# Power tables in a kernel that mixes attention with a state-space convolution: one product straight into the table, the other added to it by a GpSimd transfer

## The chip, the cores and the metric

The kernel runs on one core of a Trainium2 chip. The metric is the device time of one execution in microseconds (us), lower is better; of several timed executions the median counts. TensorE is called PE here, VectorE DVE, ScalarE ACT, GpSimd POOL, and SyncE SP. Each engine takes its instructions in order from its own queue and waits on semaphores of the others.

## The reference, cut to what matters

```python
g = sigmoid((x * gate_w).sum(-1, keepdims=True))       # x is 2048 x 512
a = softmax_attention(x, wqkv, wo)                      # 32 heads of 16, 2048 keys
logdA, dB = dt * (A_re + 1j*A_im), dt * (B_re + 1j*B_im)  # 512 channels x 128 states
P = jnp.exp(logdA[:, :, None] * l)                      # powers 0..2047 of lambda = exp(logdA)
K = einsum("dn,dnl,dn->dl", Cc, P, dB).real             # a long filter for every channel
b = causal_convolution(x, K) + x * Dskip
out = g * a + (1 - g) * b
```

The filter is applied in chunks of 64 time steps. For that the kernel needs, for each channel and state, the complex powers of lambda from 0 to 63 (times a constant): the power table, real and imaginary part, 512 channels x 128 states x 64 powers.

## The kernel before, in words

**A planner.** The program is not written out as a list. `record` builds it from threads (Python generators) that yield segments with an engine, a cost in us and a priority. For each of the NG = 683 groups of the attention (loop at line 1716) the planner places one exponential on ACT, then the score products of the next group, and then `Sched.fill` (line 372) puts in every segment of other threads that fits by its model of the engines: `op` (line 199) and `dma` (line 224) carry modelled cost and latency, `ready` (line 156) adds a margin of DMARG = 2.4 us (or PTM = 5.0) to the end of a transfer before anything that needs it is placed. The result is a fixed order for each engine; on the chip only semaphores and that order count. A first pass finds the first and last group in which each tile is used, `place` (line 526) packs the tiles into SBUF (tiles whose spans do not meet may share bytes), and a second pass replays the log with the waits that the packing adds.

**Attention.** A group is three score tiles of 128 keys x 512 queries in one of two PSUM tensors SC0 and SC1 (`qk`, line 890). `ex` (line 905) applies exp on ACT to the whole group (128x1536) or, where the third tile is given to DVE, to two tiles (128x1024). There are 2048 tiles. A *set* (`decide`, line 799; `bits`, 941; `batch`, 951) is one quad of four tiles that DVE takes instead of ACT, one tile from each of four successive groups: for each tile one operation from PSUM (line 945, tile DZ), and for each set two operations over all four tiles (line 956, tiles DU and DZ). A set starts only if its group lies in one of the windows WIN (first group, last group, sets in flight, key lists), if the key tile is in the lists VKT, and if DVE has been idle enough: by the model, idle time of DVE since the last sets (at most DVCAP = 2.0 us is kept) must reach the price that DVQ names. The price before is 0.5 us until the mark S15, then 1.0 until scan0, then 0.5 until scan1, then 0.0.

**The state-space part** fills the gaps. `params` (line 1074) makes powers of lambda and the factors D16, D32, D48 (one tile for each quarter of the channels, every factor stored twice in a row). `base` (line 1173) makes the powers 0 to 15 of each quarter in tile B16. `table` (line 1211) goes through 8 pairs of blocks of 32 channels. For a pair it copies B16 into the table tile PT (two copies, line 1227), and for each of the three factors and both parts it makes two products into tt1 and tt2 (line 1234) and their sum or difference into PT (line 1239): 2 + 3 x 2 x 3 = 20 operations of DVE. These product and sum operations go through the helper `tt`, so the profile has them on line 1006. Then SP stores both blocks of PT to DRAM (ptd, line 1244). The next pair waits for the marks K of both blocks, which `kstage` (line 1265) sets: PE multiplies PT with weights (line 1273), DVE copies the result to Kst (1277, 1278), SP stores it (1282). `qload` (line 1252) loads the stored table transposed, `sstage` (line 1288) makes the chunk states SG (it may start at the group SGAT = 175 for the first half of the channels, at 315 for the second; POOL clears the head of SG, line 1296), `scan` (line 1317) runs the recurrence over 32 chunks on DVE in two halves that end with the marks scan0 and scan1, and `ystage` (line 1384) makes the output of the convolution from SG and the table. S15 is the end of `sstage` of the last block. At the end of `emit` (line 244) SP waits for the last value of each DMA semaphore (line 272).

The line of the table that matters, with `ti` one of tt1 and tt2:

```python
tt("DVE", ti,                       B16 part xr, D part yr, ALU.mult ...)      # twice
tt("DVE", PT at 16 * m, t1, t2,     ALU.add if part else ALU.subtract ...)     # once
```

Of the kernel before, what the change touches and what calls it, by code (L numbers as in the profile page):

```python
# [2 lines left out]

# [10 lines left out]
P = 128  # L14
S = 2048
# [12 lines left out]
XAT = "base0"  # L28
# [10 lines left out]
SGAT = (175, 315)  # L39
# [50 lines left out]
class Prog:  # L90
# [133 lines left out]
    def dma(self, eng, fn, R=(), W=(), c=.45, lat=3.0, m=DMARG):  # L224
# [4 lines left out]
        k = self.dnext  # L229
        self.dnext = (k + 1) % NDSEM  # L230
# [13 lines left out]
    def emit(self, nc, es):  # L244
        sem = {e: es.enter_context(nc.semaphore("s_" + e)) for e in ("PE", "ACT", "DVE", "POOL")}
        dsem = [es.enter_context(nc.semaphore(f"s_d{k}")) for k in range(NDSEM) if self.dn[k]]
# [9 lines left out]
        def stream(eng):  # L256
            def body(e):
# [11 lines left out]
                if eng == "SP":  # L269
                    for k in range(NDSEM):  # L270
                        if self.dn[k]:
                            e.wait_ge(dsem[k], 16 * self.dn[k])
# [142 lines left out]
def declare(nc, es):  # L415
# [64 lines left out]
    for n in (16, 32, 48):  # L480
        for k in range(4):
            sb(f"D{n}.{k}", 4 * P)
# [8 lines left out]
    sb("tt1", 2 * CB * 16)  # L491
    sb("tt2", 2 * CB * 16)
# [33 lines left out]
def place(nc, bufs):  # L526

    base, end = (nc.sbuf_base + 31) // 32 * 32, nc.sbuf_usable_end
    sbs = [b for b in bufs.values() if b.kind == "sb" and b.first is not None]

    def fit(order):
        done, top = [], base
        for b in order:
            n = (b.nbytes() + 31) // 32 * 32
            busy = sorted((o.lo, o.hi) for o in done if o.first <= b.last + 1 and b.first <= o.last + 1)
            at = base
            for lo, hi in busy:
                if at + n <= lo:
                    break
                at = max(at, hi)  # L540
            b.lo, b.hi = at, at + n
            top = max(top, b.hi)
            done.append(b)
        return top

    best, seed = None, 1
    for k in range(400):
        def rank(b):
            nonlocal seed
            seed = (seed * 1103515245 + 12345) % 2 ** 31  # L550
            w = seed / 2 ** 31 * (0 if k < 2 else .8)
            return (-(b.last - b.first > 300) if k % 2 else 0, -b.nbytes() * (1 + w * 2) * (b.last - b.first + 20) ** (w if k >= 2 else 0))
        order = sorted(sbs, key=rank)
        top = fit(order)
        if best is None or top < best[0]:
            best = (top, order)
    k = 0
    while best[0] > end and k < 12000:
        k += 1
        order = list(best[1])  # L560
        for _ in range(1 + k % 3):
            seed = (seed * 1103515245 + 12345) % 2 ** 31
            b = order.pop(seed // 7 % len(order))
            seed = (seed * 1103515245 + 12345) % 2 ** 31
            order.insert(seed // 7 % (len(order) + 1), b)
        top = fit(order)
        if top <= best[0]:
            best = (top, order)
    assert best[0] <= end, (best[0] - end, live(sbs))
    fit(best[1])  # L570
# [41 lines left out]
def record(nc, p, B, ins):  # L612
# [461 lines left out]
    def params():  # L1074
# [69 lines left out]
        for o, x, y in (("L16", "L8", "L8"), ("L32", "L16", "L16"), ("L48", "L16", "L32"), ("MU", "L32", "L32")):  # L1144
            yield from cmul("DVE", o, x, y)
            if o != "MU":
                for k in range(4):
# [3 lines left out]
                       [(l, 0)], [(d, 0)], c=.34)  # L1151
        sch.mark("D48")
# [58 lines left out]
    def table():  # L1211
        yield ("AFTER", "D48")
        t1, t2 = B["tt1"], B["tt2"]
        H10 = dv(1024, 2)
        for pb in range(NBLK // 2):
# [8 lines left out]
            W = [(PT, 0, blks[0]), (PT, 1, blks[1])]  # L1224
            for i in range(2):
                yield ("DVE", .4)
                op("DVE", lambda v, i=i, b0=b0, B16=B16: v.tensor_copy(PT(i * PTN, [[CB * T, 2], [T, CB], [1, 16]]),
                                                                     B16(b0 + i * CB * 16, [[2048, 2], [16, CB], [1, 16]])), bk, [W[i]], c=.34)
# [589 lines left out]
```

## Time and profile before

| what | value |
|---|---|
| median of the timed executions | 838.77 us (838.6 to 840.81, 3 runs) |
| span of the profiled execution, first to last instruction | 837.7 us; the page gives no other time of that execution |
| median less that span | 1.07 us |
| PE busy | 698.3 us, 83% |
| DVE busy | 783.3 us, 94%, 1344 instructions |
| ACT busy | 819.1 us, 98%, 695 instructions |
| POOL busy | 11.0 us, 1%, 13 instructions |
| mean granted clock of TensorE | 0.991 |
| transfers | 94.90 MB, 49.6% of the 16 DMA engines' span on the SP queue |

An operation's mean duration in the rows includes the part that overlaps with its neighbour on the same engine; busy time divided by the count is what one costs in a row of many.

### The profile page before, as it was taken

What the parts mean: (1) busy time and instruction counts of PE and PEld (TensorE: products, weight loads), DVE (VectorE), ACT (ScalarE), POOL (GpSimd) and SP (SyncE); (2) the same over time, 40 slices, a digit from 0 to 9 for tenths busy, and PEclk for the clock granted to TensorE, in tenths of its full rate; (3) what the DMA queues carried; (4) which work ended last, traced back from release to release, by engine and by line L of the source; (5) the groups of instructions that cost most, each with busy time, mean ns of one, the idle gap of its engine ahead of it and who ended that gap; (6) DMA issues with size and microseconds to landing.
All of it is one profiled execution on the core that took longest, in us unless ns stands there. A gap on an engine that the chain in (4) does not pass through costs nothing.

```text
span 837.7 us, 21043 instructions
## 1 busy us (share of the span) xinstructions
PE 698.3 (83%) x8982; PEld 253.4 (30%) x8982; DVE 783.3 (94%) x1344; ACT 819.1 (98%) x695; POOL 11.0 (1%) x13
## 2 busy tenths in 40 slices
PE   7877777787679888887788887788897779999996
PEld 3232332122122332332232332244342224333332
DVE  5799999999889998999999999999899999999996
ACT  7999999999999999999999999999999999999996
POOL 4000000000000000000000000000000000000000
PEclk9999999999999999999999999999999999999999
DMA  9650044792361976873392846045564414544113
GB/s 207 142 83 10 23 77 92 202 228 57 128 177 46 223 123 179 119 205 67 139 144 40 143 67 143 1 108 136 140 148 109 115 54 110 135 99 132 34 45 101
DMA packets 248465, 94.90 MB, mean 113 GB/s; under 512 B 223156, under 2 KB 235316, under 8 KB 246324
## 3 DMA queue, kind: packets, MB, share of 16 engines
q1 hardware_dynamic: 246500, 92.51, 49.6%
q8 instruction: 70, 1.15, 0.5%
q10 hardware_dynamic: 1872, 1.05, 0.5%
q14 instruction: 23, 0.19, 0.1%
HBM read 33.08 MB, written 35.01 MB: 81 GB/s over the span
## 4 chain that ended last, share of the span: by engine, by line
ACT 83%; DVE 7%; PE 5%; DMA 3%; SPq 0%; issue 0%; ACTq 0%; DVEq 0%
ACT ET L909 83%; PE SC L628 2%; PE OA L628 2%; DVE tt L1006 2%; DMA gm_ptd<-PT 2%; DVE PT L1006 1%; DMA Wk<-in_A_wqkv_dram 1%; DVE DZ L945 1%; PE MB L628 1%; DMA XY<-gm_xrd 1%; DVE DZ L956 0%; DVE s L1336 0%; DVE OT L980 0%; DVE s L1338 0%; SPq L1371 0%
## 5 line engine op out<-in xcount | busy, mean ns | idle before, releaser
L909 ACT ACTIVATE ET<-SC 128x1536 bf16<-128x1536 f32 (+1 forms) x683 | 810.8, 1537 | 5.9 <-PE SC L628 3.6
L628 PE MATMUL SC<-Qm,KT 32*128 32x512 bf16 x2048 | 276.1, 387 | 122.4 <-ACT ET L909 107.7
L628 PE MATMUL OA<-wm 128*32 128x512 bf16 (+3 forms) x1374 | 204.1, 365 | 1.2 <-DVE wm L681 1.2
L945 DVE TENSOR_SCALAR DZ<-SC 128x512 uint16<-128x512 f32 x256 | 170.1, 684 | 10.3 <-PE SC L628 9.4
L628 PE MATMUL OA<-ET,VE 128*32 128x512 bf16 x1792 | 179.7, 394 | 0.0
L628 PEld LDWEIGHTS SC<-Qm,KT 32*128 32x128 bf16 x2048 | 70.9, 91 | 339.8 <-ACT ET L909 303.1
L628 PEld LDWEIGHTS OA<-ET,VE 128*32 128x32 bf16 x1792 | 45.7, 93 | 102.0 <-issue 97.6
L628 PEld LDWEIGHTS OA<-wm 128*32 128x32 bf16 (+2 forms) x1374 | 54.6, 95 | 25.9 <-issue 17.7
L956 DVE TENSOR_SCALAR DZ<-DZ 128x2048 uint16<-128x2048 uint16 x64 | 43.8, 684 | 3.0 <-PE OA L628 2.7
L1309 DVE TENSOR_SCALAR SG<-MB 128x512 bf16<-128x512 f32 x64 | 43.7, 684 | 3.0 <-DMA gm_ptd<-PT 1.7
L956 DVE TENSOR_SCALAR DU<-DZ 128x2048 uint16<-128x2048 uint16 x64 | 43.1, 684 | 0.1
L628 PE MATMUL MB<-X,Qt 128*128 128x64 bf16 x512 | 42.1, 244 | 1.2 <-DVE SG L1309 1.2
L1344 DVE TENSOR_TENSOR G<-s,s 128x512 f32<-128x512 f32 x60 | 41.3, 688 | 1.1
L1338 DVE TENSOR_TENSOR s<-G,MU 128x512 f32<-128x512 f32 x60 | 41.1, 684 | 0.0
L1341 DVE TENSOR_TENSOR s<-s,SG 128x512 f32<-128x512 f32 x60 | 41.0, 683 | 0.0
L1336 DVE TENSOR_TENSOR s<-G,MU 128x512 f32<-128x512 f32 x60 | 40.9, 682 | 0.0
L628 PEld LDWEIGHTS MB<-X,Qt 128*128 128x128 bf16 x512 | 28.8, 116 | 20.0 <-issue 20.0
L1006 DVE TENSOR_TENSOR ft<-FP,L 128x1024 f32<-128x1024 f32 (+1 forms) x32 | 34.4, 1086 | 0.2
L1006 DVE TENSOR_TENSOR PT<-tt,tt 128x1024 bf16<-128x1024 bf16 x48 | 32.9, 685 | 0.5
L628 PEld LDWEIGHTS MB<-Py,SG 128*32 128x32 bf16 x1024 | 27.8, 168 | 6.8 <-issue 4.1
L628 PE MATMUL MB<-Py,SG 128*32 128x64 bf16 x1024 | 28.6, 231 | 0.0
L1347 DVE CAST SG<-G 128x512 bf16<-128x512 f32 x60 | 25.3, 422 | 1.1
(167 smaller groups left out, 613.9 us busy)
## 6 DMA issues: line engine op xcount, KB each, us to landing
gm_ptd<-PT SPq DMA_DIRECT2D x16, 1024.0 KB, 5.9
Py<-gm_ptd SPq DMA_DIRECT2D x32, 512.0 KB, 4.3
gm_kpd<-Kst SPq DMA_DIRECT2D x16, 256.0 KB, 3.1
Tt<-gm_kpd SPq DMA_DIRECT2D x128, 32.0 KB, 3.2
gm_xrd<-in_A_x_dram SPq DMA_DIRECT2D x1, 2048.0 KB, 13.7
gm_xcd<-wm SPq DMA_DIRECT2D x4, 512.0 KB, 10.4
gm_xcd<-XR SPq DMA_DIRECT2D x32, 64.0 KB, 1.9
Wo<-in_A_wo_dram SPq DMA_DIRECT2D x4, 512.0 KB, 3.8
```

What stands on the lines that cost most here:

```text
L628: op("PE", lambda t: t.matmul(out(), lhsT(), rhs(), start=start, stop=stop, skip_group_check=True, **kw), R, W, c=c, lat=.15, a=a, cfg=cfg)
L909: op("ACT", lambda a: a.activation(ET(512 * e, [[1, 512 * n]]), sc(0, [[1, 512 * n]]), AF.Exp, scale=DH ** -0.5), [(sc, i, g) for i in ran ...
L945: op("DVE", lambda v: v.tensor_scalar(z.u16(512 * k, [[1, 512 * n]]), sc(512 * na, [[1, 512 * n]]), XS, XB, ALU.mult, ALU.add), [(sc, na + ...
L956: op("DVE", lambda v: v.tensor_scalar(t.u16(0, [[1, 2048]]), z.u16(0, [[1, 2048]]), float(STEP[k][0]), None, ALU.add), R, W, c=.07 + 2048 ...
L1006: op(eng, lambda v: v.tensor_tensor(o(), a(), b_(), f), R, W, c=c)
L1309: op("DVE", lambda v, kh=kh, part=part: v.tensor_scalar(sg(2 * SGH + SGH * part + CB * k8 + 16 * kh, [[2 * SGH, 32], [1, 16]]), MB(0, [[16 ...
L1336: op(e, lambda v: v.tensor_tensor(s2(0, W), G(0, W), MU(d0, [[0, 2], [1, 256]]), ALU.mult), key("G", "MU"), [(s2, 0)], c=F5)
L1338: op(e, lambda v: v.tensor_tensor(s3(0, W), G(256, [[-256, 2], [1, 256]]), MU(D + d0, [[D, 2], [1, 256]]), ALU.mult), key("G", "MU") + [(M ...
L1341: op(e, lambda v, so=so: v.tensor_tensor(s2(0, W), s2(0, W), sg(so, [[SGH, 2], [1, 256]]), ALU.add), [(s2, 0)] + ks, [(s2, 0)], c=F5)
L1344: op(e, lambda v: v.tensor_tensor(G(0, [[1, 512]]), s2(0, [[1, 512]]), s3(0, [[1, 512]]), ALU.add), [(s2, 0), (s3, 0)], [(G, 0)], c=F5)
L1347: op(e, lambda v, so=so: v.tensor_copy(sg(so, [[SGH, 2], [1, 256]]), G(0, W)), key("G"), ks if c < NCH - 2 else [(sg, k, (h, 'G')) for k i ...
```

## The change

1. `table` makes 2 + 12 operations of DVE for a pair instead of 20. PT is laid out by part and then by block. For each part the products with the real part of the base go into PT itself, those with the imaginary part into a tile PU (PU0 for the real part of the table, PU1 for the imaginary). tt1, tt2 and the sums are gone. For each part and block a transfer issued by POOL adds 2048 columns of PU to PT (512 KB each, 4 for a pair, 32 in all).
2. The difference needs a negated factor: each D tile grows by half, and after each copy into it POOL multiplies the imaginary part by -1 into the new third (12 operations over 256 columns). POOL also clears PU0 and PU1 once (4096 columns each), since their first 16 powers are added too.
3. The transfers of POOL have a semaphore each, beside the 56 that the others share in turn. `kstage` and the store of the table wait for the adding transfers; the store takes two runs of 4 KB from each partition instead of one of 8 KB.
4. The planner's constants: `sstage` may start at groups 217 and 335 instead of 175 and 315; the windows for sets open at group 159 instead of 170, and that with four in flight and both key lists at 520 instead of 540; the prices are 1.0, 1.5, 0.75 and 0; up to 4.0 us of idle time are kept; the DVE steps of `batch` have priority 2 instead of 1; the turning of x starts at group 100 instead of at the mark base0, the first transposed loads at group 150.
5. `place` is a new search (random moves with a falling tolerance for overflow) that packs the tiles anew; tiles share other bytes than before.

```diff
-SGAT = (175, 315)
+SGAT = (217, 335)
...
-VSAT = (158, 500)
-WIN = ((170, 475, 2, 1), (475, 540, 3, 1), (540, 678, 4, 2))
-DVQ = (("scan1", 0.0), ("scan0", 0.5), ("S15", 1.0), (None, 0.5))
+VSAT = (157, 519)
+WIN = ((159, 475, 2, 1), (475, 520, 3, 1), (520, 678, 4, 2))
+DVQ = (('scan1', 0), ('scan0', 0.75), ('S15', 1.5), (None, 1.0))
...
-DVCAP = 2.0
-BUP = 1
+DVCAP = 4.0
+BUP = 2
...
-        k = self.dnext
-        self.dnext = (k + 1) % NDSEM
+        if eng == "POOL":
+            k = len(self.dn)
+            self.dn.append(0)
+        else:
+            k = self.dnext
+            self.dnext = (k + 1) % NDSEM
...
-                    for k in range(NDSEM):
+                    for k in range(len(self.dn)):
                         if self.dn[k]:
                             e.wait_ge(dsem[k], 16 * self.dn[k])
...
+                    yield ("POOL", .5)
+                    op("POOL", lambda g, d=d: g.tensor_scalar(d(4 * P, [[1, 2 * P]]), d(2 * P, [[1, 2 * P]]), -1.0, None, ALU.mult), [(d, 0)], [(d, 1)], c=.5)
...
+        for k in range(2):
+            yield ("POOL", 1.)
+            op("POOL", lambda g, k=k: g.memset(B[f"PU{k}"](0, [[1, PL]]), 0.0), [], [(B[f"PU{k}"], 0)], c=3.)
...
-                    for ti, xr, yr in ((t1, 0, part), (t2, 1, 1 - part)):
-                        yield ("DVE", H10)
-                        tt("DVE", lambda ti=ti: ti(0, [[16, 2 * CB], [2, 8], [1, 2]]),
...
-                    tt("DVE", lambda part=part, m=m: PT(part * CB * T + 16 * m, [[PTN, 2], [T, CB], [1, 16]]),
-                       lambda: t1(0, [[CB * 16, 2], [16, CB], [1, 16]]), lambda: t2(0, [[CB * 16, 2], [16, CB], [1, 16]]),
-                       ALU.add if part else ALU.subtract, [(t1, 0), (t2, 0)], W, H10)
+            for part in range(2):
+                PU = B[f"PU{part % 2}"]
+                order = [(n, m) for m in range(1, 4) for n in (1, 0)] if part == 0 or 2 == 2 else [(0, 1), (0, 2), (0, 3), (1, 1), (1, 2), (1, 3)]
+                for n, m in order:
+                    Dm = B[f"D{16 * m}.{qr}"]
+                    o, at, W = (PT, part * PL, WP[part]) if n == 0 else (PU, 0, [(PU, 0)])
+                    yr = part if n == 0 else (2, 0)[part]
                     yield ("DVE", H10)
+                    tt("DVE", lambda o=o, at=at, m=m: o(at + 16 * m, [[T, 2 * CB], [2, 8], [1, 2]]),
...
+                for i, blk in enumerate(blks):
+                    yield ("POOL", 1.)
+                    dma("POOL", lambda e, i=i, part=part, PU=PU: e.dma_start(PT(part * PL + i * CB * T, [[1, CB * T]]), PU(i * CB * T, [[1, CB * T]]), accum_op=ALU.add),
+                        [(PU, 0)], [(PT, (i, part), blk)], c=1.1, lat=5.)
...
-        yield ("AFTER", f"S{blk - 2}" if blk >= 2 else "base0")
+        yield ("AFTER", f"S{blk - 2}" if blk >= 2 else "g150")
```

More of the change, by code (lines that the diff above doesn't have):

```diff
@@ L529, in place @@
     sbs = [b for b in bufs.values() if b.kind == "sb" and b.first is not None]
+    n, cap = len(sbs), end - base
+    size = [(b.nbytes() + 31) // 32 * 32 for b in sbs]
+    near = [[j for j in range(n) if j != i and sbs[j].first <= sbs[i].last + 1 and sbs[i].first <= sbs[j].last + 1] for i in range(n)]
+    rnd = random.Random(1)
     def fit(order):
[L532 to L538, printed above, removed]
-                    break
[L540 to L569, printed above, removed]
```

68 lines of the change are left out of this document (47 added, 21 removed).

## The prediction

> **What bounds the kernel now.** First the busy shares and the shares of the chain that ended last, from the page.
>
> ```profile
> PE 698.3 (83%) x8982; PEld 253.4 (30%) x8982; DVE 783.3 (94%) x1344; ACT 819.1 (98%) x695; POOL 11.0 (1%) x13
> ...
> ACT 83%; DVE 7%; PE 5%; DMA 3%; SPq 0%; issue 0%; ACTq 0%; DVEq 0%
> ```
>
> ACT is the bound: 819.1 of 837.7 us, and 83% of the last chain. POOL is free. DVE is full too, and that matters because it takes score tiles off ACT. So I next read where DVE still has room, in the table of busy time by stretch (us from the start: stretch, length, then PE, PEld, DVE, ACT, POOL, granted clock, DMA share, GB/s). I chose the cuts at the first set, the start and middle of the scan, and its end.
>
> ```profile
> 0.00:60.00 60.00, 47.61 (x424) 19.03 (x424) 44.32 (x86) 54.74 (x45) 9.95 (x11) 1.00 0.77 151
> 60.00:215.00 155.00, 123.01 (x1248) 40.11 (x1244) 150.92 (x237) 154.29 (x117) 0.00 (x0) 0.98 0.41 94
> 215.00:390.00 175.00, 147.34 (x1711) 49.95 (x1711) 162.36 (x280) 174.18 (x151) 0.53 (x1) 0.99 0.66 149
> 390.00:520.00 130.00, 107.33 (x1262) 38.97 (x1258) 126.76 (x220) 129.26 (x106) 0.52 (x1) 1.00 0.59 112
> 520.00:690.00 170.00, 139.69 (x2245) 53.00 (x2245) 165.19 (x296) 168.45 (x140) 0.00 (x0) 0.99 0.40 100
> 690.00:830.00 140.00, 130.41 (x2095) 51.33 (x2096) 130.76 (x224) 137.02 (x140) 0.00 (x0) 1.00 0.39 94
> ```
>
> Length less DVE's busy time is its idle time: 4.1, 12.6, 3.2, 4.8 and 9.2 us in the five stretches from 60 on. ACT hardly idles in any. The same stretches for the tile DU alone (columns PE, PEld, DVE) count the sets, one DVE operation for each:
>
> ```profile
> 215.00:390.00 175.00, 6.44 (x64) 1.71 (x64) 10.73 (x16) 0.99 0.66 149
> 390.00:520.00 130.00, 2.72 (x28) 0.74 (x28) 4.76 (x7) 1.00 0.59 112
> 520.00:690.00 170.00, 3.90 (x40) 1.13 (x40) 6.94 (x11) 0.99 0.40 100
> 690.00:830.00 140.00, 12.20 (x124) 3.26 (x124) 20.67 (x31) 1.00 0.39 94
> ```
>
> Sixteen sets before 390 us, 18 while the scan runs, 31 after it (an operation across a cut counts twice). DVE time is the currency: whoever frees it can buy sets, and sets shorten ACT. The price of one is in the groups of instructions by shape, of ACT from 20 to 180 us (no sets) and from 690 to 830 us, then of DVE over the whole span:
>
> ```profile
> L909 ACT ACTIVATE ET<-SC 128x1536 bf16<-128x1536 f32 x121 | 162.7, 1996 | 0.0
> ```
>
> ```profile
> L909 ACT ACTIVATE ET<-SC 128x1024 bf16<-128x1024 f32 x121 | 113.3, 1152 | 1.7 <-PE OA L628 1.6
> ```
>
> ```profile
> L945 DVE TENSOR_SCALAR DZ<-SC 128x512 uint16<-128x512 f32 x256 | 170.1, 684 | 10.3 <-PE SC L628 9.4
> ...
> L956 DVE TENSOR_SCALAR DZ<-DZ 128x2048 uint16<-128x2048 uint16 x64 | 43.8, 684 | 3.0 <-PE OA L628 2.7
> ...
> L956 DVE TENSOR_SCALAR DU<-DZ 128x2048 uint16<-128x2048 uint16 x64 | 43.1, 684 | 0.1
> ...
> L1006 DVE TENSOR_TENSOR PT<-tt,tt 128x1024 bf16<-128x1024 bf16 x48 | 32.9, 685 | 0.5
> ```
>
> A three-tile exponential costs ACT 162.7 / 121 = 1.345 us, a two-tile one 113.3 / 121 = 0.936 us, so a set of four tiles saves 4 x 0.409 = 1.63 us of ACT. It costs DVE (170.1 + 43.8 + 43.1) / 64 = 4.02 us.
>
> **The change part by part: the sums.** The last row above is what goes: 48 sums, 32.9 us of DVE. The 96 products and the 16 copies stay, same count and size. Products that write PT at a stride of 64 instead of tt densely are not in the trace as such; the sums wrote PT just so and took 685 ns against some 684 for the products, so I add nothing (bounds 0 and, should each product cost one more tenth, 96 x 0.07 = 7 us).
>
> **What the freed time buys.** Taking n more sets, DVE has 1.63n less span and 4.02n more work: n = (32.9 - i) / 5.65, where i is the idle time that DVE gains. With i = 0 it is 5.8 sets and 9.5 us; but the change raises the price of a set. Up to the mark S15 a set must find 1.0 us of idle time instead of 0.5. From 215 to 520 us 23 sets had 12.6 + 3.2 = 15.8 us of idle. At 1.0 they need 23, less 4.0 kept from before the window: 19, so about 3 more. Some four extra sets need 4 more. From 520 to 690 us 11 sets pay 0.25 more each: 3. So i = 10 and n = 22.9 / 5.65 = 4.05, that is 68 sets and 6.6 us less on ACT. The ends: i = 0 or, if the larger credit and the earlier window use up holes that now lie idle (12.6 us before 390), i = -10 with 7.6 sets and 12.4 us; on the other side i = 30, half a set, nothing.
>
> **Where the freed time lies.** The instructions of single lines and tiles, with their first and last start: the first exponentials, the sums, the evacuations of `sstage`, the starts of the two scans, the units of `ystage` after scan1.
>
> ```profile
> L909 ACT ACTIVATE ET<-SC x2: 1442/1446/1451, 11.6 to 13.4; 128x1536 bf16<-128x1536 f32 x2
> ...
> L1006 DVE TENSOR_TENSOR PT<-tt,tt x48: 648/687/693, 125.7 to 403.4; 128x1024 bf16<-128x1024 bf16 x48
> ...
> L1309 DVE TENSOR_SCALAR SG<-MB x64: 631/684/693, 267.5 to 512.6; 128x512 bf16<-128x512 f32 x64
> ...
> L1333 DVE CAST G<-SG x2: 421/426/431, 387.4 to 545.1; 128x512 f32<-128x512 bf16 x2
> ...
> L1420 DVE TENSOR_TENSOR Yst<-MB,gt x16: 384/415/426, 693.7 to 807.1; 128x256 bf16<-128x256 f32 x16
> ```
>
> Sums stood on DVE from 125.7 to 403.4 us, about a third before the window opens at group 159 (11.6 + 159 x 1.345, near 225 us, against 240 for group 170). Before that the bases and parameters take the time; DVE idled only 4.1 us there. After it the sets must, two in flight. At 4.02 us each, 24 sets in 175 us are 96 us of DVE, and 162.4 - 16 x 4.02 = 98 us is the other work there, some 20 us of it sums: it fits, with little to spare.
>
> **The added work of POOL.** Its nearest rows, by tile and from the timeline of POOL, and the transfers from the page (KB each, us to landing):
>
> ```profile
> L1296 POOL MEMSET SG<- x2: 524/524/525, 243.4 to 412.5; 128x512 bf16 x2
> ```
>
> ```profile
> 1.46 7.68 POOL L698 MEMSET VE<- 128x2240 bf16 x4 [0.32 <-DVE piota L686]
> ```
>
> ```profile
> gm_ptd<-PT SPq DMA_DIRECT2D x16, 1024.0 KB, 5.9
> Py<-gm_ptd SPq DMA_DIRECT2D x32, 512.0 KB, 4.3
> ...
> gm_xcd<-wm SPq DMA_DIRECT2D x4, 512.0 KB, 10.4
> ...
> gm_od<-AO SPq DMA_DIRECT2D x3, 512.0 KB, 2.6
> ```
>
> The two clearings of PU are 2 x 4096 columns at 7.68 / 4 / 2240, 3.5 us each; the 12 negations lie between 0.1 and 0.53 us each. All of it is hidden by an engine that is 99% idle, and stands early, behind the D copies. If a negation held up DVE, at most 12 x 0.53 = 6.4 us of DVE, one set, would go; I take 0.
>
> No adding transfer stands in the trace. Between 512 KB stored in 2.6 us and 512 KB in small pieces in 10.4 us I take 5.9 us, the row of the 1 MB store, since an addition has to read what it changes and moves that much. The planner allows 1.1 + 5.0 + 2.4 = 8.5 us from issue before it places a reader. So nothing waits at 5.9, and at 10.4 each reader waits 1.9. On the page "DMA: Bandwidth & Descriptors" of the Trainium skill, section "Anatomy of one DMA — SWDGE (gpsimd) path", a transfer from GpSimd is fitted as 2.0 us plus its bytes over 436 GB/s; as an estimate from that page 512 KB take 3.2 us, additions are not priced there, and by it the sum stays as it is.
>
> **The waits that are added.** A pair's order was products, sums, store; now an addition lies between products and everything that reads PT. Three queues hold a waiter. On PE it is the kstage products, and behind them score products, for which ACT waits. On SP it is the store of the table, and behind it the loads of Qm, then transposed loads. On DVE it is the next pair's copy into PT, already late once:
>
> ```profile
> 228.46 0.42 DVE L1227 COPY PT<-B 128x1024 bf16<-128x1024 bf16 x1
> 231.24 0.43 DVE L1227 COPY PT<-B 128x1024 bf16<-128x1024 bf16 x1 [2.36 <-DMA gm_ptd<-PT]
> ```
>
> A pair took that long from its store to its successor that 2.36 us of DVE idled; with an addition ahead of the store such holes grow by 5.9 us where nothing else is ready. From the window's opening a set can fill them, so I leave this inside i = 10. On POOL the additions wait for products, and the clearing of SG, which waited here for bytes of other tiles, now stands among them:
>
> ```profile
> POOL SG L1296 <- DVE tt L1006: 232.5, 1, 232.5
> POOL SG L1296 <- DMA gm_ptd<-PT: 168.6, 1, 168.6
> ```
>
> If it waits, additions behind it wait, then PE. The planner knows this wait, so 0.
>
> **The later start of the chunk states.** Group 217 instead of 175 is 42 x 1.345 = 56 us later by groups, near 295 us against 240. What is late next is the first scan, which began at 387.4. Eight blocks at (512.6 - 267.5) / 16 = 15.3 us end near 417 us at the latest, 30 us later, and near 400 if the table, which is ahead by then, was what paced them. A scan that shares DVE with no table pays it back. I put nothing of it into i, but the end has little room (a rival below).
>
> **The end.** SP's waits on DMA semaphores at the end of the program, and its own wait there:
>
> ```profile
> L272 SPq EVENT_SEMAPHORE  x28: 17/28/28, 834.5 to 837.3; - x28
> ```
>
> ```profile
> SPq L272 <- DMA out_dram<-fo: 1.2, 2, 0.8
> ```
>
> 28 instructions for 56 semaphores take 2.8 us, 1.2 of it waiting, so 0.06 us each. The change adds 32 semaphores, 16 instructions: 0.9 us (0 if they pass while the last store is still on its way, 1.6 at 0.1).
>
> **Sum.** -6.6 + 0.9 = -5.7 us against the span of 837.7, 832.0; with the 1.07 us between span and median, 833.1, rounded 833. No stall of ACT is counted.
>
> **Rivals.**
> *Idle time is not bought dearer* (i from 0 to -10): the prices only spread sets out, and the new packing takes waits away. -8.6 to -11.5 us, 830 to 827. For it: 12.6 us of idle before 390. Against: prices are doubled, and the additions make holes. It shares the sign of the forecast.
>
> *The gain goes into holes* (i near 25 to 30): the chain of a pair gets longer, the store still takes 5.9 us, sets are limited to two in flight, and the freed time before the window finds no work. 0 to 1.4 sets, -1.4 to +0.9: 838.
>
> *Slower: the additions land after their allowance, and PE stands.* Each pair has one moment in which kstage is placed as soon as the planner believes in the landing. If a landing is late by d, PE stands d, ACT d less its lead. The rows of waits show what lead there is:
>
> ```profile
> PEld SC L628 <- ACT ET L909: 313.4, 563, 1.2
> ...
> PE SC L628 <- ACT ET L909: 113.8, 282, 0.9
> ```
>
> PE waits for ACT by about one microsecond at most, so a stall beyond 1 us is ACT's. At a landing of 11.5 us, d = 3, eight pairs cost 8 x 2 = 16 us, and blocks on SP as many again in the worst case: +10 to +20, 849 for one stall each. It decides from d = 1.7 (8 x 0.7 = 5.7), a landing of 10.2 us, just at the slowest row. For it: the DMA share is 0.66 from 215 to 390 already, and 32 transfers of 512 KB at half of 5.9 us each are 94 us of 16 engines, a third more. The rule of the Trainium skill that speaks for it is on the page "SBUF — State Buffer", section "Who interferes with whom": GpSimd cannot write the descriptors of its transfers while DVE runs an operation that takes both port pairs, as the additions over four tiles may be. This case's rows can only say how often: two operations of 0.68 us a set are 22 us of those 175, so a transfer is met one time in eight and held 0.7 us at most, within the allowance.
>
> *Slower at the end: the late chunk states* push scan1 past 705 us; the 16 units of `ystage` that took 113 us after it then end past 820, and the rest of the output after it: 842. The freed DVE time speaks against it.
>
> **How the numbers follow.** Forecast 833 (830 to 836): 0.48. Idle time not dearer: 0.18. Gain into holes: 0.14. Late additions: 0.13, late end: 0.07. A measurement of this kernel tells 0.3%, 2.5 us, from no change. Faster is then 0.66, same 0.14, slower 0.20. The range goes from 825, near the end of the second case, to 843, which takes in the late end and leaves out most of the late additions.
>
> **What would show each step.** In the profile after: no group PT<-tt,tt; two-tile exponentials near 272 (257 before), since 683 groups stay; DVE's busy share no lower than about 93% with 68 sets. From 215 to 390 us more sets than 16. No wait of PE or SP for a PT addition over 1 us; the rows of waits would name the transfer. ACT idle still some 18 us in all. I am wrong if the count of two-tile exponentials stays at 257 (the holes), or if ACT's idle time grows by more than 5 us (the stalls).

## Result and the profile after

| | before | after |
|---|---|---|
| median of the timed executions | 839.72 us (838.6 to 844.03, 6) | 863.93 us (857.15 to 872.53, 6) |
| ratio, with its 95% interval | 1 | 1.0273 [1.0233, 1.0314] |
| profiled execution; its span | span 837.7 us | 859.22 us; span 857.2 us |
| granted clock | 0.991 | 0.973 |

The kernel became slower by 2.7%; 833 us was forecast, and the range ended at 843. Executions of one and the same changed kernel lie up to 2% apart, so a ratio below leaves out those more than 1.5% above their kernel's fastest, and where a kernel has no ratio its medians are given with all executions.

The page of the kernel after, busy time and the shares of the last chain:

```profile
PE 702.9 (82%) x8989; PEld 253.4 (30%) x8989; DVE 771.9 (90%) x1314; ACT 814.0 (95%) x695; POOL 63.7 (7%) x59
...
ACT 70%; SPq 10%; DVE 9%; DMA 5%; PE 4%; issue 1%; DVEq 0%
```

ACT is busy for 5.1 us less, as forecast in kind; but it idles 857.2 - 814.0 = 43.2 us where it idled 18.6. 24.6 - 5.1 = 19.5 us is the whole difference of the spans. SP's queue and DMA, 3% of the chain before, are now 15%. The groups of ACT by shape (busy us, mean ns, idle before):

```profile
L910 ACT ACTIVATE ET<-SC 128x1536 bf16<-128x1536 f32 x414 | 566.5, 1692 | 15.8 <-PE SC L629 13.7 <-PE OA L629 2.0
L910 ACT ACTIVATE ET<-SC 128x1024 bf16<-128x1024 f32 x269 | 258.9, 1183 | 13.2 <-PE SC L629 13.1
```

269 two-tile exponentials instead of 257: 67 sets, 68 were forecast. The table by stretches (columns as in the prediction):

```profile
60.00:215.00 155.00, 119.18 (x1164) 39.28 (x1168) 144.15 (x222) 143.86 (x109) 33.09 (x26) 0.93 0.48 105
215.00:390.00 175.00, 136.82 (x1565) 43.17 (x1557) 142.07 (x241) 159.47 (x139) 20.09 (x21) 0.95 0.93 199
390.00:520.00 130.00, 107.96 (x1264) 38.74 (x1261) 123.99 (x213) 129.52 (x109) 0.52 (x1) 0.99 0.69 124
```

Length less ACT's busy time is 11.1, 15.5 and 0.5 us, where it was 0.7, 0.8 and 0.7: everything is lost before 390 us, while the table is made. There the DMA engines are busy to 0.93 instead of 0.66, and the granted clock is lower. The rows of ACT's timeline with the long stalls (start, us, operation, idle before and what ended it):

```profile
123.52 1.45 ACT L910 ACTIVATE ET<-SC 128x1536 bf16<-128x1536 f32 x1 [2.95 <-PE SC L629]
...
200.57 4.25 ACT L910 ACTIVATE ET<-SC 128x1536 bf16<-128x1536 f32 x3 [6.39 <-PE SC L629]
...
251.10 1.02 ACT L910 ACTIVATE ET<-SC 128x1024 bf16<-128x1024 f32 x1 [5.70 <-PE SC L629]
...
260.29 1.02 ACT L910 ACTIVATE ET<-SC 128x1024 bf16<-128x1024 f32 x1 [5.34 <-PE SC L629]
```

Each is followed back by reading what PE, then DVE, then SP did just before. For the first, the timelines of DVE and of POOL:

```profile
116.00 3.59 DVE L1043 TENSOR_SCALAR MU<-pt 128x512 f32<-128x512 f32 x1
```

```profile
112.36 6.96 POOL L1220 MEMSET PU<- 128x4096 bf16 x2
```

The DVE operation took 3.59 us beside the second clearing of PU; operations of that shape beside it in time took 0.42. For the stalls at 200 and 251 us, the timeline of DVE and that of SP:

```profile
196.03 0.76 DVE L1233 COPY PT<-B 128x1024 bf16<-128x1024 bf16 x2 [7.40 <-DMA gm_ptd<-PT]
...
238.49 0.76 DVE L1233 COPY PT<-B 128x1024 bf16<-128x1024 bf16 x2 [10.41 <-DMA gm_ptd<-PT]
```

```profile
169.89 4.36 SPq L1472 DMA_TRANSPOSE XR<-gm_xrd  x2
...
187.88 2.85 SPq L1253 DMA_DIRECT2D gm_ptd<-PT  x2
...
239.62 22.29 SPq L1265 DMA_TRANSPOSE Qt<-gm_ptd  x8
```

DVE, in order, stands at the next pair's copy into PT until the last pair's table is stored; behind the copy stand the score tiles that it takes for ACT and the transposes of outputs, for which PE waits, and then ACT. The store of the first stall is late because on SP it comes behind transposed loads: two of them took 4.36 us, and SP then waited 6.1 us for them to land. This row of SP's timeline before has the usual time:

```profile
106.63 2.50 SPq L1463 DMA_TRANSPOSE XR<-gm_xrd  x2
```

The second stall's later store was issued at 233.31 us, behind more such loads (two of them 5.24 us). The eight Qt loads of 22.29 us come after it on SP and hold up the next pair's store, for which DVE then waited 1.4 us only. The stall at 260 us is PE's own wait on an addition. The waits of DVE, PE and SP that this rests on (us, times, longest), and the transfers (KB each, us to landing):

```profile
DVE PT L1233 <- DMA gm_ptd<-PT: 19.8, 4, 10.4
```

```profile
PE MB L629 <- DMA PT<-PU: 4.8, 1, 4.8
```

```profile
SPq L266 <- DMA PT<-PU: 17.3, 5, 10.0
SPq L266 <- DMA XR<-gm_xrd: 12.9, 4, 6.1
```

```profile
q0 software_dynamic: 4608, 16.78, 10.7%
...
PT<-PU POOLq DMA_DIRECT2D x32, 512.0 KB, 7.8
gm_ptd<-PT SPq DMA_DIRECT2D x16, 1024.0 KB, 5.8
Qt<-gm_ptd SPq DMA_TRANSPOSE x64, 5.1
XR<-gm_xrd SPq DMA_TRANSPOSE x16, 3.7
```

q0 is POOL's queue: 16.78 MB took 10.7% of 16 engines over 857.2 us, 91.7 us of all of them. The transposed loads land in 5.1 and 3.7 us; 4.2 and 2.7 before.

### The profile page after: what moved, and what is told of

The parts are those of the page before. It is cut to its first block, busy times and chain, and to the rows that moved or that the text cites. A ratio compares the mean times of both kernels' runs of the same rounds, so it can differ in the third digit from the quotient of the medians.

```text
span 857.2 us, 21118 instructions
## 1 busy us (share of the span) xinstructions
PE 702.9 (82%) x8989; PEld 253.4 (30%) x8989; DVE 771.9 (90%) x1314; ACT 814.0 (95%) x695; POOL 63.7 (7%) x59
## 3 DMA queue, kind: packets, MB, share of 16 engines
q0 software_dynamic: 4608, 16.78, 10.7%
## 4 chain that ended last, share of the span: by engine, by line
ACT 70%; SPq 10%; DVE 9%; DMA 5%; PE 4%; issue 1%; DVEq 0%
ACT ET L910 70%; SPq L1265 4%; DMA XR<-gm_xrd 2%; DMA gm_ptd<-PT 2%; PE SC L629 2%; PE OA L629 1%; SPq L1476 1%; SPq L1472 1%; DVE DZ L946 1%; DMA xT<-in_A_x_dram 1%; PE MB L629 1%; DVE ft L1007 1%; SPq L644 1%; DVE PT L1007 1%; DVE PU L1007 1%
## 5 line engine op out<-in xcount | busy, mean ns | idle before, releaser
L946 DVE TENSOR_SCALAR DZ<-SC 128x512 uint16<-128x512 f32 x268 | 178.4, 684 | 16.3 <-PE SC L629 15.7
L957 DVE TENSOR_SCALAR DZ<-DZ 128x2048 uint16<-128x2048 uint16 x67 | 46.4, 692 | 2.5 <-PE OA L629 2.4
L1249 POOL DMA_DIRECT2D PT<-PU x32 | 30.4, 1089 | 235.9 <-DVE PT L1007 222.3
L957 DVE TENSOR_SCALAR DU<-DZ 128x2048 uint16<-128x2048 uint16 x67 | 45.4, 689 | 0.1
L629 PE MATMUL OA<-DZ,VS 128*32 128x512 bf16 x268 | 26.4, 385 | 1.8 <-DVE DZ L957 1.7
```

Source lines behind the costliest of these rows:

```text
L629: op("PE", lambda t: t.matmul(out(), lhsT(), rhs(), start=start, stop=stop, skip_group_check=True, **kw), R, W, c=c, lat=.15, a=a, cfg=cfg)
L946: op("DVE", lambda v: v.tensor_scalar(z.u16(512 * k, [[1, 512 * n]]), sc(512 * na, [[1, 512 * n]]), XS, XB, ALU.mult, ALU.add), [(sc, na + ...
L957: op("DVE", lambda v: v.tensor_scalar(t.u16(0, [[1, 2048]]), z.u16(0, [[1, 2048]]), float(STEP[k][0]), None, ALU.add), R, W, c=.07 + 2048 ...
L1249: dma("POOL", lambda e, i=i, part=part, PU=PU: e.dma_start(PT(part * PL + i * CB * T, [[1, CB * T]]), PU(i * CB * T, [[1, CB * T]]), accum ...
```

## The experiments

All start from the kernel after. In the first group the order of every queue is kept, so that only one cost changes. Theory: the freed DVE time works as forecast, and the bytes of the additions take it back. Rivals: it is lateness of the additions; it is POOL holding DVE; it is the plan. Two edits come again and again:

```diff
# tiny: an addition moves 64 columns, not 2048
-PT(part * PL + i * CB * T, [[1, CB * T]]), PU(i * CB * T, [[1, CB * T]]), accum_op=ALU.add
+PT(part * PL + i * CB * T, [[1, T]]), PU(i * CB * T, [[1, T]]), accum_op=ALU.add
# short clearing: only the first 16 of 64 columns of PU
-g.memset(B[f"PU{k}"](0, [[1, PL]]), 0.0)
+g.memset(B[f"PU{k}"](0, [[T, 2 * CB], [1, 16]]), 0.0)
```

**e1_tiny: the tiny edit.**

> The changed kernel with the same order on every engine, but each adding transfer adds only the first 64 of its 2048 columns (most of the second products is left out of the table). Theory A (the additions and their traffic land too late for the order, and the queues of SP, DVE and PE stand): landing falls from 7.8 us to under 4, the idle time of ACT before its exponentials falls from 29.0 to 8 to 13 us, and the time from 864 to 843 to 849. Theory B (GpSimd's own work holds DVE): within 3 us of the changed kernel. Theory C (the new order and its constants are bad by themselves): at least 858.

837.09 us (834.86 to 838.43), ratio 0.9968 [0.9949, 0.9987]. With all waits, instructions and semaphores, but without the bytes, the change is a gain of 0.3%, and better than the 843 to 849 us expected for it. What is left of the long stalls is the first one, with the DVE operation at 3587 ns.

**e2_memset: the short clearing.**

> The changed kernel with the same order, but GpSimd clears only the 16 of every 64 columns of PU that the products do not write (1024 columns instead of 4096, the result is the same). Theory B: the DVE operation on MU that took 3.59 us takes 0.4 again, the ACT wait of 3.5 us near 120 us goes, the time falls by 3 to 5 us to about 860; the rest stays. Theory A or C alone: the DVE operation stays long or the time does not change.

870.37 us (866.26 to 875.59), ratio 1.0376 [1.0316, 1.0437]. The operation is back at 414 ns and the stall at 123 us is gone, but nothing is gained: ACT's idle time on score tiles is 33.7 us. The others are no smaller for it. The same kernel took 863.94 us when it was run again (e25 below), so its distance to the kernel after, either way, is no larger than the spread of one kernel's executions.

**e8_tinymem: both edits.**

> Same order, both edits: additions of 64 columns only (most of the second products is left out) and the short clearing. Theories A and B together: ACT idle before exponentials 5 to 9 us, time 838 to 845, no slower than the kernel before by more than 0.5%. Theory C: at least 852.

833.48 us (831.59 to 834.53), ratio 0.993 [0.9909, 0.9952]: the forecast's 833. Against e1 the clearing costs 3.6 us, once the other stalls are away. Its stretch from 215 to 390 us, the wait of DVE, and the eight Qt loads that took 22.29 us after:

```profile
215.00:390.00 175.00, 147.75 (x1738) 49.46 (x1744) 153.16 (x264) 172.78 (x154) 20.62 (x22) 1.00 0.73 162
```

```profile
DVE PT L1233 <- DMA gm_ptd<-PT: 5.4, 2, 5.2
```

```profile
223.77 10.99 SPq L1265 DMA_TRANSPOSE Qt<-gm_ptd  x8
```

ACT idles 2.2 us here instead of 15.5, and the loads issue in half the time, in a stretch with a DMA share of 0.73 instead of 0.93. In the time of the eight loads alone the engines are busy throughout in both kernels (last columns: granted clock, DMA share, GB/s), after and here:

```profile
239.62:261.91 22.29, 11.38 (x99) 2.38 (x99) 14.90 (x31) 9.98 (x11) 4.28 (x4) 0.62 1.08 173
```

```profile
223.77:234.76 10.99, 8.30 (x107) 2.50 (x104) 10.77 (x23) 10.99 (x11) 4.28 (x4) 1.00 1.04 164
```

So the mean share of a stretch does not show where the engines are full. There the same loads take longer beside the larger additions.

**e9_half: 1024 of 2048 columns, short clearing.**

> Order of the changed kernel, short clearing, each addition over half of its columns (1024 of 2048; the other half of the second products is left out). With 64 columns this kernel took 833.5 us, with all 870.4. Theory A1 (the loss grows with the bytes): landing 5 to 6 us, time 842 to 856. Theory A2 (there is a threshold, the allowance of 8.5 us of the plan, and below it nothing is lost): 832 to 838.

839.79 us (838.22 to 844.82), ratio 1.0011 [0.9988, 1.0033]. Half the bytes, 6.3 us of loss, with one stall of 5.63 us behind a DVE wait on the store of 10.3. It fell between the two expected ranges. The loss grows with the bytes, and faster than they do: all of them, with this clearing, cost 23 us at the least (856.6 us, the lowest of e25 and e2, less 833.48).

**e11_late: as e8, but each pair of additions held back by a 16 KB transfer, some 4 us.**

```diff
+prog.dma("POOL", 16 KB from wm to unused DRAM)   # ahead of every second addition, which waits for it
```

> Order of the changed kernel, short clearing, additions of 64 columns only (the rest is left out), and ahead of each two of them a transfer of 16 KB to unused DRAM whose landing they wait for, so that they land some 4 us later without moving more bytes, about as late as the full additions. Theory L: 845 to 868, PE waits on the additions again. Theory T: 833 to 839.

834.72 us (833.09 to 836.8), ratio 0.9939 [0.9913, 0.9964]. Lateness without bytes costs 1.2 us, less than the two ratios' intervals can tell. PE's wait on additions rises to 3.2 us, and ACT idles 4.6. As the main cause, lateness falls; the bytes stay.

**e10_traffic: as e8, and behind each addition 512 KB to unused DRAM for which nobody waits.**

```diff
+prog.dma("POOL", 512 KB from wm to unused DRAM)   # behind every addition
```

> Order of the changed kernel, short clearing, additions of 64 columns only (the rest of the second products is left out), and behind each of them one transfer of 512 KB from GpSimd to unused DRAM that nothing waits for. Theory T (traffic alone: it holds up the transposes, stores and loads of the other queue, and those hold up SP, DVE and PE): 848 to 868, with the transposes XR landing near 3.7 us and the DVE copies into PT waiting over 10 us. Theory L (the late landing of the additions themselves, for which PE and SP wait): 832 to 838.

846.89 us (844.46 to 850.18), ratio 1.0092 [1.0057, 1.0127]: 13.4 us for bytes alone. The waits of DVE and the Qt loads:

```profile
DVE PT L1239 <- DMA gm_ptd<-PT: 18.3, 3, 9.9
```

```profile
231.67 15.24 SPq L1271 DMA_TRANSPOSE Qt<-gm_ptd  x8
```

So the late store of the table needs no late addition: foreign bytes are enough.

**e20_late_traffic: e10 and e11 together.**

> The changed kernel's order, short clearing, additions of only the first 64 of 2048 columns (the other columns are left out of the sum), each pair of additions held back by a 16 KB transfer, and behind each addition a 512 KB transfer of GpSimd to unused DRAM for which nobody waits. Apart, the two cost 1.2 us and 13.4 us above 833.5. If they only add up: 846 to 850. If lateness costs more among crowded transfers (interaction): 853 to 865, with DVE's wait on the table's store above 20 us.

847.11 us (846.02 to 851.36), ratio 1.0096 [1.0066, 1.0126]. The two only add up; lateness among plain bytes costs nothing more.

**e3_plain and e22_plainmem: plain copies of all bytes, with the long and the short clearing.**

```diff
-..., accum_op=ALU.add)
+...)
```

> The changed kernel with the same order, each adding transfer replaced by a plain copy of the same bytes from the same queue (the table then holds only the second products). If theory A holds because an addition reads, adds and writes: landing falls from 7.8 to 4 or 5 us and the time to 846 to 854. If it holds because of the bytes and the crowded DMA engines: landing stays above 6.5 us and the time within 4 us of the changed kernel.

> The changed kernel's order, short clearing, and plain copies of GpSimd in place of the additions (the table then holds the second products instead of the sums), all bytes and all waits. If adding itself is dear: 846 to 852, since it then differs from the run with traffic alone by about 4 us of landing only. If waits and bytes together make the loss, whatever the transfer does: 855 to 866.

854.61 us (849.32 to 859.56), ratio 1.0184 [1.0116, 1.0252], and 851.1 us (846.3 to 864.52), 1.0108 [1.0061, 1.0155]. Every reader waits for the whole transfer, but it is no addition, and the time is near that of bytes alone; the second one's lies in the range expected if adding itself is dear. Its queue and landing:

```profile
q0 software_dynamic: 4608, 16.78, 6.0%
...
PT<-PU POOLq DMA_DIRECT2D x32, 512.0 KB, 4.8
```

The same 16.78 MB: 6.0% of 849.1 us is 50.9 us of all engines, against 91.7 as additions.

**e21_adding: as e8, and behind each addition a second adding transfer of 512 KB into PU.**

> As the former without the holding back, and in place of the 512 KB transfer to DRAM one of the same bytes that adds constants to the tile PU in SBUF, which nobody writes or reads before the next pair's products (its result is not used; the sums of the other columns are left out). If an adding transfer occupies the DMA engines more than a plain one: above 850, up to 862, against 846.9 for the plain transfer to DRAM, with a share of GpSimd's queue near 10% against 6%. If only the bytes count: 844 to 849.

935.42 us (932.64 to 938.0). This one says nothing of the price, and its expectation left out why: both transfers were given one region of PU, so each waited for the other.

```profile
POOL PT L1254 <- DMA PU<-wm: 96.4, 16, 8.4
POOL PU L606 <- DMA PT<-PU: 89.2, 32, 5.8
```

**e23_adding2 and e24_copying2: the same with a region of its own, 496 KB from KT, once added and once copied; e25_memset2: the complete change with the short clearing, beside them.**

```diff
+prog.dma("POOL", PU columns 64 to 2047 (+)= KT columns, accum_op=ALU.add or none)   # behind every tiny addition
```

> The changed kernel's order and short clearing, additions of only the first 64 of 2048 columns (the rest is left out of the sum), and behind each a second adding transfer of GpSimd of 496 KB, from KT to the other columns of PU, whose result is not used and for which nobody waits before the next pair's products, some 30 us later. If adding is dear by the time that it holds the DMA engines: GpSimd's queue takes 9 to 11% of them, and the time is 852 to 866. If the loss needs readers that wait for the large transfer itself: 844 to 850, whatever the share.

> As the former with plain copies of the same 496 KB to the same place. Both theories: 842 to 849, a share of GpSimd's queue near 6%.

> The changed kernel complete, in its order, with the short clearing alone, once more: 860 to 872. Its distance to the first run of this call is what waiting for the large additions costs beyond their traffic.

Added: 875.0 us (864.93 to 885.04), ratio 1.0329 [1.0264, 1.0394], above both expected ranges. Copied: 853.75 us (852.03 to 855.26), 1.0166 [1.0128, 1.0205]. Complete: 863.94 us (856.6 to 871.95). The queues and landings of the first and of the second:

```profile
q0 software_dynamic: 9216, 16.78, 12.5%
...
PU<-KT POOLq DMA_DIRECT2D x32, 496.0 KB, 8.0
```

```profile
q0 software_dynamic: 7168, 16.78, 8.2%
...
PU<-KT POOLq DMA_DIRECT2D x32, 496.0 KB, 5.0
```

Additions whose result nobody uses cost no less than the complete change, and 1.6% more than copies of the same bytes to the same place. The shares hold the 32 small additions too (1.3% in e8). The copies came out 5 us above what both theories had. One thing isn't kept apart: the small additions, for which readers do wait, stand behind the large transfers on the queue. Their median landing was 5.9 us in the first and 4.0 in the second, but single ones took up to 17.7 and 19.5, and PE waited for them, in the first and in the second:

```profile
PE MB L637 <- DMA PT<-PU: 9.7, 3, 6.5
```

```profile
PE MB L637 <- DMA PT<-PU: 12.4, 1, 12.4
```

In the second this was ACT's longest stall, 12.97 us, and most of what the copies cost there. The difference between the two can't come from it, since the copies have the longer wait of PE; DVE's wait on the table's store is 30.1 us with additions and 13.1 with copies.

**e12_truth: planned again with the landing that was measured, short clearing.**

```diff
-c=1.1, lat=5.)
+c=1.1, lat=9.)
-SGAT = (217, 335)
+SGAT = (256, 374)
```

> Complete result, planned anew: the plan takes 9 us instead of 5 for the landing of an addition (with its margin 12.5 from issue), the chunk states start at group 256 instead of 217 because the tiles would not fit otherwise, short clearing. Theory L (late against the plan): no wait of PE on an addition above 1 us, ACT idle below 12 us, time 832 to 843. Theory T: the stores and transposes are still late, 846 to 862.

863.59 us (860.67 to 874.48), ratio 1.027 [1.023, 1.031]. PE's wait on additions fell to 0.9 us, as it should, and the time stayed. One stall of 16.57 us took the place of the others, behind this row of DVE:

```profile
257.00 0.77 DVE L1233 COPY PT<-B 128x1024 bf16<-128x1024 bf16 x2 [17.79 <-DMA gm_ptd<-PT]
```

Its store stood on SP behind seven Qt loads of 11.63 us. That raised the question whether SP's queue is the whole cause.

**e17_poolstore: the 16 stores of the table on POOL's queue, the rest of the order kept, short clearing.**

```diff
+if f.__name__ == "dma" and a[3][0][0] is bufs["ptd"]:
+    a = ("POOL",) + tuple(a[1:])
```

> The changed kernel in its own order, with the short clearing of PU (870.37 in the run with that alone), and one thing turned: the 16 stores of the table are issued by GpSimd, behind the additions that they wait for, instead of by SP, where they stand behind the transposed loads. Same bytes, same additions, complete result. Theory Q (the loss comes from the store standing behind slow transposes on SP's queue, and DVE's copy behind the store): DVE's wait on the store falls from 25.7 us below 12, ACT's idle time on score tiles from 33.7 to about 15, the time to 850 (843 to 857). Theory B (the bytes themselves: a store lands as late from any queue, because the DMA engines are full): DVE's wait on the store stays at 20 us or more, and the time at 862 to 874.

857.65 us (855.61 to 879.44), ratio 1.0227 [1.0202, 1.0253]. DVE's wait on the store is gone altogether, as theory Q had it, but the time fell into neither range: it is 6 to 13 us below the two medians with the short clearing alone (e25 and e2), but their executions, from 856.6 us, overlap with its own, from 855.61, so a gain isn't shown. The next in SP's queue became the victim, the loads of Qm, behind transposed loads and `gm_xcd` stores that took 9.75 us:

```profile
PE SC L631 <- DMA Qm<-gm_qd: 19.1, 2, 13.8
```

With no transfer of POOL issued beside them, the eight Qt loads took little more than in e8:

```profile
248.25 12.33 SPq L1267 DMA_TRANSPOSE Qt<-gm_ptd  x8
```

**e14_q212, e18_early_q200, e19_early: planned again, short clearing, with the transposed loads elsewhere.**

```diff
-yield ("AFTER", f"S{blk - 2}" if blk >= 2 else "g150")
+yield ("AFTER", f"S{blk - 2}" if blk >= 2 else "g212")   # e14; g200 in e18
-XAT = 'g100'
+XAT = 'g85'        # e18, e19, and the table's store on POOL's queue
```

> The changed kernel planned again, with the short clearing and one constant turned: the first transposed loads of the table (Qm, blocks 0 and 1, eight loads) may be placed from exponential group 212 on instead of 150, so most of them leave SP's queue ahead of the later table stores. Complete result, all additions. Theory Q: the wait of DVE for the store of blocks 2 to 5 falls, ACT's idle time on score tiles falls from 27 to 34 us to about 15, and the time is 845 to 857, if the loads' later place costs nothing at the scan. Theory B: the same bytes crowd the same engines, 860 or more; a later start of the first scan (387 us before) would show as a late end besides.

> The changed kernel planned again, complete result, short clearing, and three things that take the crowd off SP in the table's stretch: the stores of the table are placed on GpSimd's queue, the transposed loads XR begin at exponential group 85 instead of 100 (about 20 us earlier), and the first transposed loads Qt at group 200 instead of 150. The same bytes move in all. Theory Q' (bytes cost through SP's slow queue: whatever stands on it behind transposes comes late, the store in the changed kernel, the loads of Qm once the store is gone from it): with the transposes apart from the additions no wait on the store, on Qm or on the additions exceeds about 4 us, ACT's idle time on score tiles is 5 to 15 us, and the time is 836 to 848. Theory B (the bytes delay by themselves, wherever they stand): a new victim takes the place of Qm, ACT idles 20 us or more, 852 to 865.

> As the kernel before it in this call, but with the first transposed loads Qt at group 150 as in the changed kernel, so that these eight loads stand among the additions again. Theory Q': some 3 to 8 us more than the former, with PE's wait on Qm or on the additions as the new idle time, 841 to 855. Theory B: no difference between the two beyond 2 us, both 852 to 865.

872.39 us (853.83 to 876.87); 877.51 us (874.13 to 890.4), ratio 1.0446 [1.042, 1.0471]; 874.16 us (869.33 to 903.79), 1.0364 [1.0343, 1.0385]. None is shown to be a gain, against theory Q for the first (though one execution of it took 853.83 us) and Q' for the others. In the third a stall of 21.93 us came from the place of the XR loads: SP waited 23.2 us for DVE's `nwi`, and the stores of Qs came behind the XR loads:

```profile
DVE Qs L719 <- DMA gm_qd<-Qs: 27.4, 3, 22.1
```

By subtraction, an estimate, its span of 877.6 would be near 856 without that stall, and e17's is 853.8. With each order something else came late first: the table's store, the loads of Qm, the stores of Qs. What made SP's wait so long in the third isn't settled; DVE's wait for the stores of Qs is as long in the second (22.3 us).

## Why the prediction was wrong

**The bound and the currency were right.** DVE time bought sets at the forecast price: 67 for 68, and 5.1 us of ACT for 6.6. Where transfers carry next to nothing and the clearing is short (e8), the kernel takes 833.48 us, ACT is busy for 6.8 us less, and DVE idles 62.3 us for 54.4, a gain of 7.9 where i = 10 was taken. The place was off. The stretches of after for the tile DU (one DVE operation for each set):

```profile
215.00:390.00 175.00, 6.12 (x60) 1.61 (x60) 10.27 (x15) 0.95 0.93 199
390.00:520.00 130.00, 3.90 (x40) 1.06 (x40) 6.71 (x10) 0.99 0.69 124
520.00:690.00 170.00, 3.11 (x32) 0.85 (x32) 5.54 (x8) 1.00 0.53 121
690.00:850.00 160.00, 13.35 (x136) 3.64 (x136) 22.88 (x34) 1.00 0.36 90
```

Fifteen sets lie before 390 us, where sixteen did: the freed time of the table's own stretch, for which the window was opened earlier, bought none there, and the gain comes after it. Products written into the table directly cost the same 0.69 us.

**The step that failed: "I leave this inside i = 10", and "No stall of ACT is counted".** The copy into PT was quoted with its 2.36 us, and its growth by 5.9 us for each pair was put into idle time that sets fill. DVE takes its queue in order: what stands behind the copy can't fill the hole, and PE and ACT wait for just that. The wait is now 19.8 us in four pieces, and DVE idles 85.3 us: i is 30.9, not 10. Twenty-five microseconds of new idle time of ACT stand in the place of nothing; more than 5 was the forecast's own sign of being wrong. The 5.9 us stood for an addition's landing ahead of the store, and that isn't what makes the wait long: held back by some 4 us without their bytes (e11), additions cost about a microsecond. The store comes late because of the bytes.

**The size that wasn't priced was in the forecast.** The late-additions rival had "94 us of 16 engines, a third more", and 91.7 were measured. That they agree is luck: it took half of a landing of 5.9 us, and an addition took 91.7 / 32 = 2.9 us of all engines out of a landing of 7.8. It served there only to make a landing late. What it did was to slow all others: Qt and XR loads, the stores, whatever SP issued behind them. With nothing else changed, the medians go from 837.09 us (e1) through 854.61 (plain waited copies, e3) to 863.93: 17.5 us for the bytes, with what readers wait longer for them, and 9.3 for adding. By ratios, plain waited copies cost 2.2% (e3 over e1) and 1.8% (e22 over e8, some 15 us; between the ends of the intervals 9 to 21). Adding instead of copying costs 0.9% (after over e3; between the ends of the intervals -0.2 to 2.0%) and 1.6% (e23 over e24, 14 us; 5 to 22). So the bytes' part is shown well, and that adding costs more than copying rests on the second pair and on the engines' time; its size is known only roughly.

**The landing.** 5.9 us was taken, with 10.4 as the upper bound; the median is 7.8 us, single ones took up to 12.9. The 3.2 us that the forecast estimated for a transfer without an addition lie below even the 4.8 us of a plain copy here (e22). But the rival that hung on the landing was right in its sign and in a small part: PE waited for an addition once, 4.8 us, and ACT's stall behind it is 5.34 us of the 24.6; later additions without bytes cost 1.2 us; a plan that allows for the landing took that wait away and gained nothing. The wait varies between executions of one kernel: 10.0 us in e2, 1.8 in e25.

**POOL.** The clearing was sized right (3.5 us each) and wrongly put as hidden: it held a DVE operation for 3.2 us, 3.6 us of time by e1 and e8. The page "SBUF — State Buffer" of the Trainium skill, section "Who interferes with whom", says that a DVE operation in a two-port mode and GpSimd exclude one another, and that who issues first keeps the ports for its whole instruction. The trace agrees, with 3.59 us for 0.42, ending 0.3 us behind the second clearing, and with 0.41 in e2; that this operation ran in such a mode no row says. The forecast had weighed this direction for the negations alone, at 6.4 us at most, and not for the clearing. Negations took 0.84 to 1.83 us against at most 0.53, at no cost that shows.

**The rest.** The later chunk states cost nothing, as forecast: from 390 us to 520 ACT idles 0.5 us, 0.7 before. Semaphores at the end: 4.3 us for 44 instructions, 1.7 of it waiting, 0.06 each, as forecast.

**What stays open.** Why the stall of an order lies where it lies, and why executions of one order differ by 2%, isn't settled; nor what adding costs beyond copying, more closely than the two pairs above. A second buffer for PT, which would let DVE go on, wasn't tried. No version here with the complete result beats the kernel before: the complete change lies above it in every order.

## What to carry to other kernels

Work that moves from a full engine to transfers isn't free because the DMA engines idle a third of the time on average: price it in engine time in its own stretch, look for the moments in it in which the engines are already full, and ask whose transfers share them and who stands in order behind those. Judge a hole on an in-order engine by what is queued behind the waiting instruction, not by the engine's idle total. To test such a change quickly, keep the order and shrink the transfer: if the gain comes back, it is the bytes.

## What the runs showed of the hardware

- An adding transfer within SBUF occupies the DMA engines 1.8 times as long as a copy (91.7 against 50.9 us for 16.78 MB) and lands in 7.8 us instead of 4.8 (512 KB). The page "DMA: Bandwidth & Descriptors" of the Trainium skill, section "SDMA does more than copy", lists adding among the small compute units in line with a transfer's data. No run here shows the unit; the rows show only the longer time.
- POOL is busy for 0.95 us to issue an adding transfer (30.4 us for 32) and for 0.62 to issue a copy (19.8 us for 32, e22). An addition of 16 KB lands in 3.2 us (e8).
- SP's issue of the same eight transposed loads took 10.99 us beside additions of 16 KB (e8), 15.24 beside transfers to DRAM (e10), 18.00 beside plain copies (e22), 22.29 beside the full additions, and 12.33 in e17, where POOL issued nothing during them, in a stretch with a DMA share of 0.91. The copies of e24 are out of line: 28.90. Crowded engines are seen first as a slow queue.
- The granted clock fell with a stall of PE in the kernel after: behind 5.8 us without work (192 to 198 us) it was 0.50 until 210 us, 0.87 until 214 and 1.00 from there to 220, and PE's products of 128x512 took 0.60 to 0.62 us instead of 0.39 or 0.40. In the two stretches that have the stalls it is 0.93 and 0.95, where it was 0.98 and 0.99 before.
